# An attention and feed-forward kernel: the opening's copies, casts, loads and first up tiles rearranged

## The chip, the core and the metric

The kernel runs on one core of one Trainium2 chip. A core has five engines that run their own instruction streams in order: TensorE (matrix products, into PSUM), VectorE (DVE), ScalarE (ACT), GpSimd (POOL) and SyncE (SP), and they meet by semaphores. Transfers between memory and SBUF are issued by SP, ACT and POOL. PSUM has eight banks of 128 partitions x 512 floats.

The metric is the device time in microseconds of one execution, the median of the runs; lower is better.

## The reference

Attention with 16 query heads on 4 key and value heads, eight batches of 384 positions, head width 64; then a feed-forward layer with a squared ReLU over the 3,072 rows.

```python
k = np.repeat(k, 4, axis=1); v = np.repeat(v, 4, axis=1)
scores = np.matmul(q, k.transpose(0, 1, 3, 2)) / np.sqrt(64)
attn = softmax(scores)                                # over the keys
x = np.matmul(attn, v).transpose(0, 2, 1, 3).reshape(3072, 1024)
h = np.maximum(x @ w_in, 0.0)                         # w_in 1024 x 2048
out = h * h @ w_out                                   # w_out 2048 x 1024
```

Inputs and output are float32; the kernel casts to bfloat16 for its products.

## The kernel before

**Recording.** Every operation goes through `R.add` (L45): engine, function, tiles read and written, and an estimated cost. The recorder keeps an estimated clock per engine and per transfer queue (`ring`), derives from the tiles who waits for whom, and at the end emits each engine's operations in the order recorded (L78). The costs decide nothing on the chip except this order. The order on TensorE is chosen by the loop from L575: it collects candidates, each with the time at which it is estimated ready and a priority (score burst of batch 0: 0, transpose for q or k: 1, attention times V: 2, transpose of the output: 3, score burst of a later batch: 4, feed-forward piece: 5), and takes the ready one of lowest number, or the earliest.

**Attention, per batch.** Keys are copied twice side by side (`dup_k`, L253), so that a transpose gives the same keys on partitions 0 to 63 and 64 to 127, and two score products can run in two halves of the array. Keys and queries are turned by TensorE through PSUM and a DVE copy in batches 0 and 1 (`turn_k_pe` L278, `turn_q_pe` L293), by transposing transfers from SP later (`turn_k_dma`, `turn_q_dma`). A unit is one of 12 key blocks (4 heads x 3); its scores are 128 keys x 2 x 768 columns. In batch 0 ScalarE takes their exponentials in bursts of 1,024 columns from two pairs of banks, 0/1 and 2/3 (`burst_small`, L320: 18 bursts); later batches take two units at once from banks 0 to 5 (`burst_two`, L340: 3,072 columns). `expT` has room for eight units. `av` (L363) then makes eight pieces c per batch, each 18 small products with V, a reciprocal and a multiply on DVE; `turn_o_pe` (batch 0) or `turn_o_dma` gives x transposed, in eight chunks.

**Feed-forward, per batch.** 16 up tiles (`up_part`, L418: eight chunks of 1,024, then max on DVE and square on ScalarE) and six down tiles (`down_part`), all in banks 6 and 7. In batch 0 the first two up tiles are opened together and take the x chunks two by two as they come (`ffn`, L442).

**The opening.** `first_loads` (L207) brings the keys of head 0 on SP's queue, q of heads 0 to 3 and then the other keys on ACT's queue, all as float32. Everything else that is loaded is cast on the way and issued by POOL, in the order of L495 to L518: q and V of batch 0, three casts of keys, V's copy, three pieces of w_in (each serves two up tiles), batch 1's k, q, V, five pieces of w_in, batch 1's copies, w_out. TensorE warms up with 14 products of 256 columns (L523). DVE doubles the first keys and casts 512 columns of the first q, ACT casts 256 (L529 to L535).

**Preparing batch 2 and later.** `prepare` (L555) lists the key copy, the transposing transfers and V's copy. It is called when the batch before has all its scores issued and enough V pieces done (L586).

Of the kernel before, what the change touches and what calls it, by code (L numbers as in the profile page):

```python
# [8 lines left out]
class Recorder:  # L9
# [35 lines left out]
    def add(self, eng, fn, reads=(), writes=(), dma=None, cost=0.1, issue=0.1, rate=None):  # L45
# [20 lines left out]
        if dma is not None:  # L66
            self.clock[eng] = start + issue
            q = eng
            begin = max(self.ring.get(q, 0.0), start + issue + 0.8)
            self.ring[q] = begin + cost  # L70
            end = begin + cost + 1.2
        else:
            self.clock[eng] = start + cost
            end = start + cost + (0.2 if eng == "tensor" else 0.07)
# [59 lines left out]
def bass_gqa_attention__then__ffn_squared_relu_kernel(  # L134
# [65 lines left out]
    def load_k(b, after=()):  # L200
        st = b % NST
        R.add("gpsimd", lambda g: g.dma_start(  # L202
            k_st[st].ap().rearrange("p (g j) d -> p g (j d)", g=HKV),
            k[b].rearrange("g (p j) d -> p g (j d)", j=NJ)),
            reads=after, writes=[("k_st", st)], dma=f"k{st}", cost=1.3, issue=0.8)

    def first_loads():  # L207

        def keys(eng, g0, g1):
            R.add(eng, lambda e: e.dma_start(  # L210
                k_f32[:, g0 * NJ:g1 * NJ, :].rearrange("p (g j) d -> p g (j d)", j=NJ),
                k[0, g0:g1].rearrange("g (p j) d -> p g (j d)", j=NJ)),
                writes=[("k_f32", g) for g in range(g0, g1)], dma=f"kf{g0}", cost=0.4 * (g1 - g0), issue=0.4)

        keys("sync", 0, 1)
        R.add("scalar", lambda e: e.dma_start(
            q_f32[:, :, :], q[0, 0:4].rearrange("h (p j) d -> p h (j d)", j=NJ)),
            writes=["q_f32"], dma="qf", cost=1.3, issue=0.4)
        keys("scalar", 1, HKV)

    def load_v(b):
# [4 lines left out]
            writes=[("v_st", st)], dma=f"v{st}", cost=1.3, issue=0.8)  # L226

    def load_q(b, h0, h1):
# [4 lines left out]
            writes=[("q_st", st, h // 4, x) for h in range(h0, h1, 4) for x in range(2)], dma=f"q{st}_{h0}",  # L233
            cost=0.33 * (h1 - h0), issue=0.8)
# [18 lines left out]
    def dup_k(b, eng, g0=0, g1=HKV):  # L253
# [3 lines left out]
        R.add(eng, lambda e: e.tensor_copy(dst, src), reads=[("k_st", b % NST)] if b else [("k_f32", g) for g in range(g0, g1)],  # L257
              writes=[("k_dup", b % 2, g) for g in range(g0, g1)],
              cost=(0.15 * n / 3 + 0.1) if eng == "vector" else 0.33 * n)

    def aug_v(b, eng):
        R.add(eng, lambda e: e.tensor_copy(v_aug[b % 2][:, :, 0:D], v_st[b % NST][:, :, :]),  # L262
              reads=[("v_st", b % NST)], writes=[("v_aug", b % 2)], cost=0.4 if eng == "vector" else 2.0)

    def turn_k_dma(b):
        R.add("sync", lambda e: e.dma_start_transpose(  # L266
            out=kT[b % 2].ap(), in_=k_dup[b % 2].ap().rearrange("p n x d -> p (n x d)")),
            reads=[("k_dup", b % 2, g) for g in range(HKV)],
            writes=[("kT", b % 2, g) for g in range(HKV)], dma="turn_k", cost=2.0)

    def turn_q_dma(b, half):
# [4 lines left out]
            writes=[("qT", b % 2, 2 * half + i, x) for i in range(2) for x in range(2)], dma=f"turn_q{half}", cost=2.5)  # L276

    def turn_k_pe(b, g, banks):  # L278
# [9 lines left out]
        R.add("tensor", tr, reads=[("k_dup", b % 2, g), "ident"], writes=[("bank", i)], cost=0.18)  # L288
# [4 lines left out]
    def turn_q_pe(b, g, banks, t0=0, t1=6):  # L293
# [3 lines left out]
        parts = [h for h in range(2) if t0 < (4, 6)[h] and t1 > (0, 4)[h]]  # L297

        def tr(pe):
            for t in range(t0, t1):  # L300
# [8 lines left out]
              reads=[("bank", i)], writes=[("qT", b % 2, g, h) for h in parts], cost=0.07 + 0.068 * (t1 - t0))  # L309

    def score_reads(b, u, parts=(0, 1)):
        g = u // NJ
        return [("kT", b % 2, g)] + [("qT", b % 2, g, h) for h in parts]
# [5 lines left out]
    def burst_small(b, pieces, base):  # L320

        wide = 512 // len(pieces)

        def sc(pe):
            for n, (u, c0) in enumerate(pieces):
                for x in range(2):
                    m = pe.matmul(ps[:, base + x, n * wide:(n + 1) * wide],  # L327
                                  kT[b % 2][64 * x:64 * x + 64, u, :], q_cols(b, u // NJ, x, c0, c0 + wide))
            return m

        keys = [("bank", base), ("bank", base + 1)]
        R.add("tensor", sc, reads=[r for u, c0 in pieces for r in score_reads(b, u, (c0 // 512,))], writes=keys,
              cost=0.22 + 0.19)
        n, c0 = (b * NU + pieces[0][0]) % NEX, pieces[0][1]
        src = ps[:, base:base + 2, :].rearrange("p x (k c) -> p x k c", k=len(pieces))
        dst = expT[:, n:n + len(pieces), :, c0:c0 + wide].rearrange("p k x c -> p x k c")
        R.add("scalar", lambda e: e.activation(dst, src, AF.Exp, scale=0.125),  # L337
              reads=keys, writes=[("expT", (n + m) % NEX, c0 // 512) for m in range(len(pieces))], cost=0.92)

    def burst_two(b, u):  # L340

        def sc(pe):
            for k0, cols in ((0, ((0, 512), (512, 768))), (1, ((0, 256), (256, 768)))):
# [14 lines left out]
              reads=keys, writes=[("expT", (n + m) % NEX, h) for m in range(2) for h in range(2)], cost=2.63)  # L358

    def av_reads(b, g):  # L360
        return [("expT", (b * NU + g * NJ + j) % NEX, h) for j in range(NJ) for h in range(2)] + [("v_aug", b % 2), ("v_one", b % 2)]

    def av(b, c, banks):  # L363
# [12 lines left out]
        R.add("tensor", lambda pe: mm(pe, 6 * s2), reads=av_reads(b, g), writes=[("bank", i)], cost=0.285)  # L376
        yield
        R.add("tensor", lambda pe: mm(pe, 6 * s2 + 3), reads=av_reads(b, g), writes=[("bank", i)], cost=0.285)
# [11 lines left out]
    def turn_o_dma(b, g):  # L390
# [5 lines left out]
            dma=f"turn_o{o}", cost=2.0)  # L396
# [21 lines left out]
    def up_part(b, c, at, k0, k1):  # L418
        def piece():
            if k0 == 0:  # L420
                at.append(pick((6, 7)))
            i = at[0]

# [16 lines left out]
        return k1, need, (6, 7) if k0 == 0 else None, piece  # L440

    def ffn(b):  # L442

        opened = 2 if b == 0 else 0
        ats = [[] for _ in range(opened)]
        for k0 in range(0, NKC, 2):
            for c in range(opened):
                yield up_part(b, c, ats[c], k0, k0 + 2)
        for c in range(opened, NFC):
# [44 lines left out]
    first_loads()  # L494
    load_q(0, 4, 8)  # L495
# [7 lines left out]
    for g in range(1, HKV):  # L503
        dup_k(0, "gpsimd", g, g + 1)
    aug_v(0, "gpsimd")
    for i in range(3):
        load_w_in(i)
    load_k(1)
    load_q(1, 0, 8)
    load_q(1, 8, 16)  # L510
    load_v(1)
    for i in range(3, 8):
        load_w_in(i)
    dup_k(1, "gpsimd")
    aug_v(1, "gpsimd")
    for jj in range(2):
# [6 lines left out]
    def warm_up(pe):  # L523
        for _ in range(14):
            m = pe.matmul(bank(7)[:, 0:256], warm[:, 0:128], warm[:, :])
        return m

    R.add("tensor", warm_up, reads=["warm"], writes=[("bank", 7)], cost=2.9)
    dup_k(0, "vector", 0, 1)  # L529
    q_to = q_st[0][:, 0:4, :].rearrange("p h e -> p (h e)")  # L530
    q_from = q_f32.ap().rearrange("p h e -> p (h e)")
    R.add("vector", lambda e: e.tensor_copy(q_to[:, 0:512], q_from[:, 0:512]),
          reads=["q_f32"], writes=[("q_st", 0, 0, 0)], cost=0.6)
    R.add("scalar", lambda e: e.copy(q_to[:, 512:768], q_from[:, 512:768]),
          reads=["q_f32"], writes=[("q_st", 0, 0, 1)], cost=0.4)  # L535
# [4 lines left out]
    for u in range(NU):  # L540
        smalls.append([(u, 0)])
        if u % 2 == 1:
            smalls.append([(u - 1, 512), (u, 512)])
    turn_q = [(0, 0, "k"), (0, 0, "a"), (0, 0, "c")]
# [5 lines left out]
    units, halves, pairs, turned, up_done = 0, set(), 0, 1, -1  # L550
# [4 lines left out]
    def prepare(b):  # L555

        chores.append(([("k_st", b % NST)], lambda: dup_k(b, "gpsimd")))
        chores.append(([("k_dup", b % 2, 0), ("k_dup", b % 2, 3)], lambda: turn_k_dma(b)))
# [13 lines left out]
    f_head = next(feeding)  # L572
    av_open = None
    margin = 0.5
    while av_q or av_open or sc_q or o_q or f_head is not None:  # L575
        now = R.clock["tensor"]
        first = bool(sc_q) and sc_q[0][0] == 0
        spare = MID if first else LOW
# [7 lines left out]
        if not chores and queued < loaded and units >= queued * NU and pairs >= queued * 8:  # L586
# [7 lines left out]
        if turn_q:  # L594
            b, g, w = turn_q[0]
            src = [("k_dup", b, g)] if w == "k" else [("q_st", b, g, h) for h in range(2) if w != "ac"[1 - h]]
            cand.append((max(R.when(reads=src), open_bank(spare)), 1, "turn"))
        if av_open is not None:
            cand.append((now, 2, "av2"))
        elif av_q:  # L600
            b, c = av_q[0]
            if units >= b * NU + (c // 2 + 1) * NJ and up_done >= b - NXT:
                cand.append((max(R.when(reads=av_reads(b, c // 2)), open_bank(spare)), 2, "av"))
        if o_q:
            cand.append((max(R.when(reads=o_q[0][2]), open_bank(spare)), 3, "o"))
        if sc_q:
            b, u = sc_q[0]
            if b == 0:
                top = max(p[0] for p in smalls[u])
                ok = all((0, p[0] // NJ, p[1] // 512) in turned_g for p in smalls[u])  # L610
                ok = ok and pairs // 2 * NJ + NEX >= top + 1
                reads = [r for p in smalls[u] for r in score_reads(0, p[0], (p[1] // 512,))]
# [3 lines left out]
            else:  # L616
                ok = ((b, (u + 1) // NJ, 1) in turned_g) if b == 1 else turned >= b
# [4 lines left out]
        if f_head is not None:  # L622
# [13 lines left out]
        if what[2] == "turn":  # L636
# [3 lines left out]
            else:  # L640
                turn_q_pe(b, g, spare, *dict(q=(0, 6), a=(0, 4), c=(4, 6))[w])
            turned_g |= {(b, g, h) for h in range(2) if w in ("q", "ac"[h])}
# [18 lines left out]
        elif what[2] == "sc":  # L661
            b, u = sc_q.pop(0)
            if b == 0:
                burst_small(0, smalls[u], 2 * (u % 2))
                halves |= {(p[0], p[1] // 512) for p in smalls[u]}
# [40 lines left out]
```

The softmax here doesn't subtract the row's maximum and nothing guards it: scores larger than these inputs give would overflow.

## Time and profile before

| | us |
|---|---|
| median of 3 runs | 432.12 (431.69 to 432.97) |
| profiled execution | 432.37 |
| its span, first to last instruction | 430.6 |
| share of the span: TensorE, DVE, ACT, POOL busy | 98%, 37%, 45%, 13% |
| up products (L426), 1,024 | 174.5 busy |
| down products (L471), 758 recorded | 167.7 busy |
| exponentials: 18 of batch 0 (L337), 42 later (L357) | 16.9 and 114.5 busy |

Busy time of an engine counts an instruction from its start to its modelled end. Products overlap on TensorE, so a product's own duration (326 ns for an up product) is longer than the distance to the next one (20.80 us for 128 of them late in the kernel, or 0.1625 each). Where work stands one behind the other, the distances between starts are used. In a timeline row the numbers are start, length, engine, line, operation, tiles written and read, shape and count; in brackets stands how long the engine was idle before it and whose end released it. The first copy of the keys and other lines on GpSimd are rough.

### The profile page before, as it was taken

The numbers are of one execution on the slowest core, as the hardware profiler recorded it, in microseconds if no ns is written. First come the engines' busy times: TensorE is split into PE (matmuls) and PEld (weight loads), VectorE is DVE, ScalarE is ACT, GpSimd is POOL, SyncE is SP. The second block draws the span as 40 slices with busy tenths as digits, with TensorE's granted clock in tenths as the row PEclk, the third lists the DMA queues.
The fourth block names the chain that finished last, engine by engine and source line by source line (L and its number), as shares of the span: only waits on it lengthen the run. The fifth ranks groups of instructions, "written<-read, shape, count | busy, mean of one in ns | idle before, by whom it ended". The sixth has DMA issues, their size and how long they took to land.

```text
span 430.6 us, 7790 instructions
## 1 busy us (share of the span) xinstructions
PE 421.8 (98%) x3428; PEld 231.6 (54%) x3454; DVE 158.9 (37%) x335; ACT 194.0 (45%) x190; POOL 55.6 (13%) x68
## 2 busy tenths in 40 slices
PE   8899999999999999999999999999999999999997
PEld 4465555465454655546555455645564455446544
DVE  3474422254233543225433243533342144224412
ACT  4937750557545576455773549540241034003300
POOL 7752002404040031004000000000000000000000
DMA  8999999999596189299553230042101100110012
GB/s 147 182 195 202 190 198 215 200 191 138 105 175 156 37 137 131 85 144 166 60 103 94 70 85 0 2 106 69 49 2 49 73 26 1 50 73 26 1 63 85
DMA packets 95331, 43.90 MB, mean 102 GB/s; under 512 B 75712, under 2 KB 89280, under 8 KB 95296
## 3 DMA queue, kind: packets, MB, share of 16 engines
q0 software_dynamic: 36544, 17.44, 32.3%
q1 hardware_dynamic: 57824, 25.27, 26.4%
q10 hardware_dynamic: 928, 0.69, 0.5%
q8 instruction: 27, 0.44, 0.4%
q14 instruction: 8, 0.07, 0.1%
HBM read 35.65 MB, written 12.58 MB: 112 GB/s over the span
## 4 chain that ended last, share of the span: by engine, by line
PE 92%; ACT 3%; DMA 2%; DVE 1%; SPq 1%; issue 1%
PE ps L426 39%; PE ps L471 37%; PE ps L347 7%; PE ps L372 7%; ACT expT L337 3%; DMA qT<-q_st 1%; DMA q_f<-in_q_dram 1%; PE ps L301 1%; SPq L266 1%; DVE o_sb L387 1%; PE ps L327 0%; PE ps L285 0%; DVE qT L308 0%; DVE y_sb L480 0%; DVE rinv L381 0%
## 5 line engine op out<-in xcount | busy, mean ns | idle before, releaser
L426 PE MATMUL ps<-xT,w_in_sb 128*128 128x384 bf16 x1024 | 174.5, 326 | 0.0
L471 PE MATMUL ps<-w_out_sb,h2T 128*128 128x512 bf16 (+2 forms) x758 | 167.7, 375 | 1.7 <-issue 0.5
L357 ACT ACTIVATE expT<-ps 128x3072 bf16<-128x3072 f32 x42 | 114.5, 2725 | 70.9 <-PE ps L347 70.0
L426 PEld LDWEIGHTS ps<-xT,w_in_sb 128*128 128x128 bf16 x1024 | 97.0, 98 | 69.3 <-issue 6.2
L436 ACT ACTIVATE h2T<-hr 128x384 bf16<-128x384 f32 x128 | 64.4, 520 | 138.0 <-DVE hr L434 137.8
L471 PEld LDWEIGHTS ps<-w_out_sb,h2T 128*128 128x128 bf16 x784 | 73.6, 98 | 87.9 <-issue 6.0
L434 DVE TENSOR_SCALAR hr<-ps 128x384 f32<-128x384 f32 x128 | 71.2, 557 | 103.9 <-PE ps L426 103.9
L480 DVE COPY y_sb<-ps 128x512 f32<-128x512 f32 (+2 forms) x49 | 33.3, 681 | 130.7 <-PE ps L471 130.7
L372 PEld LDWEIGHTS ps<-v_aug,expT 128*128 128x128 bf16 x1152 | 39.8, 97 | 6.7 <-issue 0.7
L372 PE MATMUL ps<-v_aug,expT 128*128 128x65 bf16 x1152 | 41.4, 193 | 0.3 <-ACT expT L337 0.3
L387 DVE TENSOR_TENSOR o_sb<-ps,rinv 128x384 bf16<-128x384 f32 x64 | 35.6, 557 | 2.4 <-DVE rinv L381 0.2
L347 PE MATMUL ps<-qT,kT 64*128 64x512 bf16 (+1 forms) x336 | 34.6, 325 | 0.5 <-DMA qT<-q_st 0.5
L347 PEld LDWEIGHTS ps<-qT,kT 64*128 64x128 bf16 x336 | 13.0, 94 | 21.2 <-DVE o_sb L387 4.9
L381 DVE RECIPROCAL rinv<-ps 128x6 f32<-128x6 f32 x64 | 12.1, 190 | 25.5 <-PE ps L372 25.5
L337 ACT ACTIVATE expT<-ps 128x1024 bf16<-128x1024 f32 x18 | 16.9, 1070 | 2.4 <-PE ps L327 2.2
L262 POOL COPY v_aug<-v_st 128x768 bf16<-128x768 bf16 x8 | 6.6, 830 | 83.7 <-PE ps L372 67.8
L230 POOL DMA_DIRECT2D q_st<-in_q_dram x17 | 15.0, 896 | 0.9 <-POOLq L691 0.8
L257 POOL COPY k_dup<-k_st 128x1536 bf16<-128x1536 bf16 x7 | 10.3, 1469 | 37.1 <-DMA k_st<-in_k_dram 37.1
L202 POOL DMA_DIRECT2D k_st<-in_k_dram x7 | 5.3, 757 | 39.9 <-DMA qT<-q_st 39.9
L327 PE MATMUL ps<-qT,kT 64*128 64x512 bf16 (+1 forms) x48 | 7.5, 360 | 1.8 <-ACT expT L337 1.3
L240 POOL DMA_DIRECT2D w_in_sb<-in_moe_w_in_dram x8 | 7.1, 935 | 0.0
L223 POOL DMA_DIRECT2D v_st<-in_v_dram x8 | 6.3, 788 | 0.1
(26 smaller groups left out, 42.8 us busy)
## 6 DMA issues: line engine op xcount, KB each, us to landing
out_dram<-y_sb SPq DMA_DIRECT2D x47, 256.0 KB, 2.0
q_st<-in_q_dram POOLq DMA_DIRECT2D x14, 384.0 KB, 8.9
w_in_sb<-in_moe_w_in_dram POOLq DMA_DIRECT2D x8, 512.0 KB, 16.1
w_out_sb<-in_moe_w_out_dram POOLq DMA_DIRECT2D x4, 1024.0 KB, 26.4
v_st<-in_v_dram POOLq DMA_DIRECT2D x8, 192.0 KB, 9.8
k_st<-in_k_dram POOLq DMA_DIRECT2D x7, 192.0 KB, 3.9
q_st<-in_q_dram POOLq DMA_DIRECT2D x3, 192.0 KB, 5.7
xT<-o_sb SPq DMA_TRANSPOSE x28, 2.8
```

Of the source, the lines that this page charges most:

```text
L230: R.add("gpsimd", lambda g: g.dma_start(q_st[st][:, h0:h1, :], q[b, h0:h1].rearrange("h (p j) d -> p h (j d)", j=NJ)), writes=[("q_st", st ...
L337: R.add("scalar", lambda e: e.activation(dst, src, AF.Exp, scale=0.125), reads=keys, writes=[("expT", (n + m) % NEX, c0 // 512) for m in r ...
L347: m = pe.matmul(flat[:, k0 * HC + c0:k0 * HC + c1], kT[b % 2][64 * x:64 * x + 64, u + k0, :], q_cols(b, (u + k0) // NJ, x, c0, c1))
L357: R.add("scalar", lambda e: e.activation(dst, src, AF.Exp, scale=0.125), reads=keys, writes=[("expT", (n + m) % NEX, h) for m in range(2) ...
L372: m = pe.matmul(po[:, f - 6 * s2, 0:D + 1], w, v_aug[b % 2][:, g * NJ + j, 0:D + 1], start=(j == 0), stop=(j == NJ - 1))
L381: R.add("vector", lambda e: e.reciprocal(rinv[r].ap().unsqueeze(2), po[:, :, D:D + 1]), reads=[("bank", i)], writes=[("rinv", r)], cost=0.13)
L387: R.add("vector", lambda e: e.tensor_tensor(dst, srcv, rbv, ALU.mult), reads=[("bank", i), ("rinv", r)], writes=[("o_sb", o, s2)], cost=0.48)
L426: m = pe.matmul(bank(i)[:, 0:S], w_in_sb[:, kc, c * 128:(c + 1) * 128], xT[b % NXT][:, kc, :], start=(kc == 0), stop=(kc == NKC - 1))
L434: R.add("vector", lambda e: e.tensor_scalar_max(hr[r][:, :], bank(i)[:, 0:S], 0.0), reads=[("bank", i)], writes=[("hr", r)], cost=0.48)
L436: R.add("scalar", lambda e: e.activation(h2T[b % 2][:, c, :], hr[r][:, :], AF.Square), reads=[("hr", r)], writes=[("h2T", b % 2, c)], cost ...
L471: m = pe.matmul(bank(i)[:, 0:n], h2T[b % 2][:, c, i3 * 128:(i3 + 1) * 128], w_out_sb[:, c, c0:c1], start=(c == 0), stop=(c == NFC - 1))
L480: R.add("vector", lambda e: e.tensor_copy(ysl, bank(i)[:, 0:n]), reads=[("bank", i)], writes=[("y", yb)], cost=0.08 + n / 960)
```

## The change

- **First key and q.** The first key head is copied by DVE into one half and by ACT into the other. q of heads 0 to 3 comes in two transfers on ACT's queue, and ACT casts both halves (384 columns each). The other keys move from ACT's queue to SP's.
- **Warm-up.** 22 products of 128 columns, then the first key transposes, then five more.
- **Bursts of batch 0.** Units are grouped (0), (1,2), (3,4), (5,6), (7), (8,9), (10,11). Single units and the last pair use bursts of 384 columns per half (768 in all), the other pairs two of 512 and one shared one of 2 x 256. Tiles of q and of `expT` are followed in sixths, and a V piece needs only its own three sixths of its three units.
- **POOL's order.** After batch 0's loads: w_in 0, key copy of head 1, k of batch 1, key copy of heads 2 and 3, V's copy, q of batch 1, w_in 1, V of batch 1, batch 1's key copy, w_in 2 to 5, batch 1's V copy, w_in 6 and 7, w_out.
- **Early up tiles.** Four tiles of batch 0 in lanes that take single chunks. Tiles 0 and 1 use banks 6 and 7; tiles 2 and 3 may also use banks 0 to 3 once batch 0's score bursts are all issued. Batch 1's first score burst waits until no low bank is held.
- **Planner.** Batch 1's transposes get priority 4.5 and may be placed only while fewer than six V pieces of batch 0 are done or after all of x of batch 0. Transposing transfers are priced higher while POOL's queue is full, and batch 2 is prepared only after all V pieces of batch 1. Costs of copies and loads are changed.

The diff, cut to its core:

```diff
+            if shared and self.ring.get("gpsimd", 0.0) > begin:
+                self.ring["gpsimd"] += cost
+                cost = shared
...
-        keys("sync", 0, 1)
-        R.add("scalar", lambda e: e.dma_start(
-            q_f32[:, :, :], q[0, 0:4].rearrange("h (p j) d -> p h (j d)", j=NJ)),
-            writes=["q_f32"], dma="qf", cost=1.3, issue=0.4)
-        keys("scalar", 1, HKV)
+        for g0, g1 in ((0, 1), (1, HKV)):
+            R.add("sync", lambda e, g0=g0, g1=g1: e.dma_start(
+                k_f32[:, g0 * NJ:g1 * NJ, :].rearrange("p (g j) d -> p g (j d)", j=NJ),
...
+        for n in range(2):
+            R.add("scalar", lambda e, n=n: e.dma_start(
+                q_f32[:, 2 * n:2 * n + 2, :], q[0, 2 * n:2 * n + 2].rearrange("h (p j) d -> p h (j d)", j=NJ)),
...
-        opened = 2 if b == 0 else 0
-        ats = [[] for _ in range(opened)]
-        for k0 in range(0, NKC, 2):
-            for c in range(opened):
-                yield up_part(b, c, ats[c], k0, k0 + 2)
-        for c in range(opened, NFC):
+        for c in range(0 if b else EARLY, NFC):
...
+    EARLY = 4
+    early_banks = [6, 7]
+    held = set()
+    def early(c):
+        at = []
+        return [up_part(0, c, at, k0, k0 + 1, (6, 7) if c < 2 else early_banks) for k0 in range(NKC)]
...
-    for g in range(1, HKV):
-        dup_k(0, "gpsimd", g, g + 1)
+    load_w_in(0)
+    dup_k(0, 1, 2)
+    load_k(1)
+    dup_k(0, 2, 4)
     aug_v(0, "gpsimd")
-    for i in range(3):
-        load_w_in(i)
-    load_k(1)
     load_q(1, 0, 8)
     load_q(1, 8, 16)
+    load_w_in(1)
     load_v(1)
-    for i in range(3, 8):
+    dup_k(1)
+    for i in range(2, 6):
         load_w_in(i)
-    dup_k(1, "gpsimd")
     aug_v(1, "gpsimd")
+    for i in range(6, 8):
+        load_w_in(i)
...
-    dup_k(0, "vector", 0, 1)
+    R.add("vector", lambda e: e.tensor_copy(k_dup[0][:, 0:NJ, 0, :], k_f32[:, 0:NJ, :]),
+    R.add("scalar", lambda e: e.copy(k_dup[0][:, 0:NJ, 1, :], k_f32[:, 0:NJ, :]),
...
+    for n in range(2):
+        R.add("scalar", lambda e, n=n: e.copy(q_to[:, 384 * n:384 * n + 384], q_from[:, 384 * n:384 * n + 384]),
+    turn_k_pe(0, 0, (4,))
+    warm_up(5, 0.5)
...
+    for group in ((0,), (1, 2), (3, 4), (5, 6), (7,), (8, 9), (10, 11)):
+        if len(group) == 2 and group[1] < NU - 1:
+            smalls += [[(u, 0, 512)] for u in group] + [[(u, 512, 256) for u in group]]
+        else:
+            smalls += [[(u, c0, 384)] for c0 in (0, 384) for u in group]
...
-        if not chores and queued < loaded and units >= queued * NU and pairs >= queued * 8:
+        if not chores and queued < loaded and (queued - 1, NU - 1, 5) in scored and pairs >= queued * 8 + 8 * (queued == 1):
...
+        if turn_q and (b == 0 or pairs < 6 or x_done[0] == 8):
...
+            cand.append((max(R.when(reads=src), open_bank(spare)), 3.5 * b + 1, "turn"))
...
+        for n, lane in enumerate(lanes):
+            chunks, need, banks, _ = lane[0]
+            if x_done[0] >= chunks:
...
+                cand.append((t, 5 + 0.1 * n, n))
+        if f_head is not None and not lanes:
```

## The prediction

> **What bounds the kernel now.** I read four views, in this order: busy time and chain of waits on the page, busy time by stretch, the timeline of the first 31 us, and the half-microsecond stretches for the DMA rate. First the page, its parts 1 and 4:
>
> ```profile
> PE 421.8 (98%) x3428; PEld 231.6 (54%) x3454; DVE 158.9 (37%) x335; ACT 194.0 (45%) x190; POOL 55.6 (13%) x68
> ...
> PE 92%; ACT 3%; DMA 2%; DVE 1%; SPq 1%; issue 1%
> ```
>
> TensorE is busy for 421.8 of 430.6 us. All of the chain that is not TensorE has to lie in a few places. The stretches of 5 us find them (columns: stretch, length, then busy us and count for PE, PEld, DVE, ACT and POOL, clock, DMA share, GB/s):
>
> ```profile
> 5.00:10.00 5.00, 4.53 (x34) 2.56 (x34) 2.27 (x7) 3.02 (x4) 3.63 (x7) 1.00 1.22 145
> 10.00:15.00 5.00, 3.65 (x49) 1.84 (x48) 1.86 (x5) 4.56 (x6) 5.00 (x7) 1.00 1.09 139
> 15.00:20.00 5.00, 4.77 (x80) 2.90 (x76) 3.47 (x11) 5.00 (x7) 4.25 (x5) 1.00 1.47 197
> 20.00:25.00 5.00, 4.70 (x75) 2.75 (x74) 2.04 (x7) 4.43 (x5) 1.47 (x1) 1.00 1.60 191
> 25.00:30.00 5.00, 4.50 (x73) 3.54 (x69) 3.99 (x13) 0.98 (x2) 2.61 (x4) 1.00 1.48 198
> 30.00:35.00 5.00, 5.00 (x41) 2.87 (x39) 3.21 (x9) 2.21 (x2) 4.93 (x6) 1.00 1.45 197
> ```
>
> From 30 us on TensorE is full; later only one visible stall is left (0.45 us at 77.87). Between 5 and 30 us it idles 0.47+1.35+0.23+0.30+0.50 = 2.85 us, while ScalarE is nearly full from 7 to 24.4. So this is two kernels: an opening set by ScalarE's first exponentials, then 400 us of TensorE at its limit. A microsecond won before 30 us is won at the end, since everything behind is a full queue. The timeline gives the opening's marks:
>
> ```profile
> 6.94 3.08 ACT L337 ACTIVATE expT<-ps 128x1024 bf16<-128x1024 f32 x3 [1.85 <-PE ps L327]
> ...
> 10.33 12.27 ACT L337 ACTIVATE expT<-ps 128x1024 bf16<-128x1024 f32 x13 [0.30 <-PE ps L327]
> ...
> 13.80 0.74 PE L372 MATMUL ps<-v_aug,expT 128*128 128x65 bf16 x18
> ...
> 22.25 1.47 POOL L257 COPY k_dup<-k_st 128x1536 bf16<-128x1536 bf16 x1 [3.00 <-DMA k_st<-in_k_dram]
> ...
> 28.38 0.33 PE L285 MATMUL ps<-ident,k_dup 128*128 128x128 bf16 x3
> ...
> 30.40 2.11 PE L426 MATMUL ps<-xT,w_in_sb 128*128 128x384 bf16 x12
> ...
> 77.87 0.82 PE L347 MATMUL ps<-qT,kT 64*128 64x512 bf16 x8 [0.45 <-DMA qT<-q_st]
> ```
>
> Exponentials run from 6.94 to 24.43 with one gap of 0.30. The first attention-times-V piece waits until 13.80. Batch 1's keys reach GpSimd at 22.25, so its transposes stand at 28.38 to 30.40, in a stretch where TensorE has no slack. And the load queue has a hole:
>
> ```profile
> 9.50:10.00 0.50, 0.50 (x8) 0.38 (x6) 0.28 (x1) 0.50 (x1) 0.50 (x2) 1.00 0.09 10
> 10.00:10.50 0.50, 0.50 (x5) 0.17 (x3) 0.50 (x1) 0.20 (x2) 0.50 (x1) 1.00 0.00 0
> ```
>
> The last column fell from 192 at 8.0 and is back at 193 only at 12.0: some 2.5 us without loads, because GpSimd issues the first w_in piece at 8.96, behind its key and V copies.
>
> **The first chain (copies, casts, first loads).** Before: keys land at 3.53, one DVE copy of 0.55, three transposes at 4.14; q lands whole at 4.66, cast in two parts (DVE 0.43, ACT 0.41), transposes 5.16, qT copy 5.81, scores 6.29, exponential 6.94. After: DVE and ACT copy half the first key each, 0.3 to 0.36 (the 256-column ACT cast took 0.41), so the key's transposes start near 3.95 and its copy is off DVE before q comes. ACT casts q in two halves of 384 columns, 0.41 x 384/256 less a fixed part = 0.5 each. ACT has nothing queued then but the exponentials that need these casts. The gain hangs on when the first q half lands, and here a rule speaks against the change. In the trace ACT's queue ran almost alone: of about 0.18 MB in each half microsecond from 3.0 to 4.0 all was its own, so half of q (0.2 MB) would be home some 0.5 us early, at 4.1. But now the other keys (288 KB) leave ACT's queue for SP's and run beside q. The Trainium skill, "DMA: Bandwidth & Descriptors", section on queues, rings and completion order, says that each DMA engine goes round its queues packet by packet. By it the first q half shares the 360 GB/s with the keys and lands near 4.5, the second near 5.3. I take the rule, as no row has two full hardware queues side by side. Then cast to 5.0, three transposes to 5.6, copy 0.35, a 384-column score: first exponential at about 6.5, gain 0.4 (0.8 by the lone row; 0 if both halves land together at 4.9). The second half's chain ends near 7.3, when the first exponential, 0.74 long, ends.
>
> **Exponentials.** 18 of 1024 columns become 12 of 1024 and 8 of 768, over the same 18,432 columns. In the row above 13 take 12.27, so 0.944 each; the 3072-column one takes 2.725 against 1.070, so 0.81 ns a column, and 768 columns cost 0.737. Sum 12 x 0.944 + 8 x 0.737 = 17.2, against 17.0. With gaps of 0.5 they end at 6.5+17.2+0.5 = 24.2, hardly earlier than 24.43. What changes is what can run beside them: a V piece needs only its own half columns, so the first is ready after four bursts, near 10.3 instead of 13.80, and only the last of eight is left behind the last exponential, where before two were, and their chain.
>
> **Loads.** GpSimd sat idle 1.30 us until 6.71 for the keys, so the w_in issue (0.9) hides there and fills the hole. Batch 1's keys, q and V then pass two w_in pieces on the queue: at 0.19 MB/us the keys land near 14 (before 22.2), q by 18.5 (26.3). The second w_in piece lands near 21, before the up tiles 2 and 3 that need it (after 24); later pieces come 2.5 us earlier than now, and now none is waited for. GpSimd's new wait is the batch-1 key copy ahead of four w_in issues: the queue holds work until 22 by then, so nothing starves. If that cover failed, a late w_in piece would cost its lateness one for one. Splitting the key copies differently (one group, then two, with the k load between) makes groups 2 and 3 ready near 8.9, half a microsecond later than now; their scores are due near 13.5.
>
> **Batch 1's transposes and the early tiles.** The 36 transposes cost 2.0 us at 28.38. They may now run from 16 us on, between score bursts. Isolated there they cost more (three took 0.34 busy): I add 0.4. The four early up tiles are no new work; they are the same matmuls, ready while the last V chain (reciprocal 0.20, multiply 0.56, transposes, copy 0.35) runs.
>
> **TensorE's sum.** What stands between the first transposes (4.14) and the end of batch 1's (30.40), by start-to-start times of the timeline (bursts and V pieces between 13.8 and 19 us): 18 score bursts x 0.32 = 5.8; 8 V pieces x 0.66 = 5.3; batch 0's transposes 1.3+1.08+1.01+0.84 = 4.2; eight output transposes x 0.25 = 2.0; batch 1's 2.0; 16 up matmuls x 0.1625 = 2.6. Together 21.9 of 26.3, so 4.4 us were waiting. After: 21.9 + 0.2 (two more bursts, 0.1 of weight load each) + 0.4 = 22.5 from 3.95. Waiting left: about 0.8 in the first chain, where little else is ready, and 0.4 near 11 to 13, before output and w_in are there. The same state is reached at 27.65: gain **2.75**. With only 0.5 of waiting and no dearer transposes it is 3.85; with 3.0 of waiting, because a turn stands ahead of a score in the fixed order, 0.95.
>
> **The warm-up** is shortened from 14 x 256 columns (3.17 us) to 22 and later 5 of 128. The Trainium skill, "TensorE: Matmul & The Clock Gate", Part 1, has a busy window of some 3.4 us end the half-rate clock; a shorter warm-up with a hole would then be worth another 3.4 us at half rate, at most 1.7 us. But the trace shows that today's does not reach it: three transposes take 0.50 at 8.89 and 0.34 at 10.22, so full rate comes near 9.6 from the bursts after 6.3. Those stay. I take nothing.
>
> **The stall at 77.87.** Batch 2's keys landed at 66.1, behind w_out; SP's three transposes of them follow from 69.92. The load queue is 2.5 us ahead now and the planner prices these transposes higher when GpSimd's queue is full, so batch 2's scores stand later in TensorE's order. Its start after the last V piece of batch 1 costs nothing: that piece (64.91) ended with the key copy at 66.13 anyway, and the downs of batch 0 and ups of batch 1 cover it. Worth 0.45 if gone, zero if it moves along; I take 0.45.
>
> Total 2.75+0.45 = 3.2. The profiled execution took 432.37, of which 430.6 is span and 1.77 lies around it: 429.2 by its own. The median is 0.25 lower: 428.9.
>
> **The rivals.** *All fits*: ScalarE alone sets the opening, 3.85+0.45 = 4.3, 427.8; for it, TensorE's early idle; against it, that 22.5 us of work in 23 leaves no play in a fixed order. *TensorE takes over the opening*: the added transposes share two banks and DVE with the V pieces (each V piece costs DVE 1.1 us, batch 1's copies 3.6 more; DVE was busy 3.47 of 15 to 20), bursts come late, the exponentials stretch: 0.95 and the stall stays, 431.2, or 430.7 without it. *Slower*: the clock. If the shorter warm-up and chopped bursts miss the window near 9.6 and the next two, three windows of 3.4 us at half rate cost 1.7 each, 5.1 against 3.2 won: 434.0. It decides from the second missed window; against it, TensorE is busier than before from 6 to 20.
>
> **Chances.** Forecast 0.58, all fits 0.22, TensorE takes over 0.16, clock 0.04. This measurement tells about 0.3% (1.3 us) from no change. Faster: the first two and half of the third, 0.88; same 0.08; slower 0.04. The range takes in the first two, with up to 0.8 more if the lone q row holds, and most of the third: 427.0 to 431.0.
>
> **What would show it.** First exponential at 6.3 to 6.7; 20 of them, the last ending near 24.2; no dry stretch at 9 to 11.5; batch 1's transposes before that last exponential, the first V piece near 10.3; TensorE idle from 5 to 30 down from 2.85 to about 1.3; no wait for qT near 75. I am wrong if the exponentials show gaps over 1 us, if batch 1's transposes still stand behind them, or if transposes still take 0.50 for three after 10 us.

## The result and the profile after

| | before | changed |
|---|---|---|
| median, us | 432.21 (431.69 to 432.97, 4 runs) | 430.01 (429.93 to 430.71, 4 runs) |
| ratio, 95% interval | | 0.9951 [0.9933, 0.9970] |
| span of the profiled execution | 430.6 | 428.1 |
| batch 0's exponentials: first starts, last ends | 6.94, 24.43 | 6.59, 24.63 |
| batch 1's first score burst | 32.45 | 30.60 |

The change wins 2.2 us where 3.2 were forecast; the profiled spans differ by 2.5. The page of the changed kernel, parts 1, 2 and 4 (the second row is the clock that TensorE was granted, in tenths, over 40 slices of 10.7 us; the page of before has no such row):

```profile
PE 423.2 (99%) x3467; PEld 232.2 (54%) x3467; DVE 158.8 (37%) x334; ACT 194.9 (46%) x194; POOL 55.1 (13%) x67
...
PEclk8999999999999999999999999999999999999999
...
PE 98%; DMA 1%; ACT 0%; DVE 0%; ACTq 0%; issue 0%
```

The chain is TensorE all through, and ScalarE's 3% of before has left it. That does not yet mean that ScalarE sets nothing: the chain follows what ended last, and a TensorE that is kept busy with cheap or slow work looks full. The first slice of the clock, 8, is new. The stretches show where it lies (columns as before: PE, PEld, DVE, ACT, POOL busy, clock, DMA share, GB/s):

```profile
5.00:10.00 5.00, 3.75 (x29) 1.64 (x30) 1.95 (x5) 3.92 (x6) 5.00 (x8) 0.81 1.51 182
10.00:15.00 5.00, 5.00 (x69) 3.11 (x67) 3.13 (x8) 4.41 (x5) 3.84 (x5) 0.85 1.54 191
15.00:20.00 5.00, 5.00 (x72) 2.84 (x71) 2.78 (x9) 4.84 (x7) 3.33 (x4) 1.00 1.53 196
20.00:25.00 5.00, 4.93 (x88) 3.28 (x88) 3.10 (x9) 4.50 (x6) 2.87 (x4) 1.00 1.47 198
25.00:30.00 5.00, 5.00 (x64) 3.66 (x61) 4.77 (x14) 0.39 (x1) 5.00 (x7) 1.00 1.46 197
```

TensorE's idle time from 5 to 30 us is 1.25+0.07 = 1.32, against 2.85. The dry stretch of the load queue is gone: the last column stays between 182 and 198. The clock is below 1.00 in two stretches; in steps of half a microsecond it is 1.00 up to 8.0, 0.50 from 8.5 to 11.0 and 1.00 again from 11.5. By these shares the drop lasts from about 8.1 to 11.5. The timeline of the changed kernel has the marks:

```profile
3.71 0.48 PE L286 MATMUL ps<-ident,k_dup 128*128 128x128 bf16 x3
...
5.96 0.33 PE L302 MATMUL ps<-ident,q_st 128*128 128x128 bf16 x3 [1.03 <-ACT q_st L551]
6.22 0.34 PE L328 MATMUL ps<-qT,kT 64*128 64x384 bf16 x2
...
6.59 4.35 ACT L338 ACTIVATE expT<-ps 128x768 bf16<-128x768 f32 x5 [0.78 <-PE ps L328]
...
8.30 0.61 PE L328 MATMUL ps<-qT,kT 64*128 64x512 bf16 x2
8.84 0.50 PE L286 MATMUL ps<-ident,k_dup 128*128 128x128 bf16 x3
9.27 0.61 PE L328 MATMUL ps<-qT,kT 64*128 64x256 bf16 x4
9.81 0.82 PE L302 MATMUL ps<-ident,q_st 128*128 128x128 bf16 x6
10.43 0.53 PE L286 MATMUL ps<-ident,k_dup 128*128 128x128 bf16 x3
10.89 0.61 PE L328 MATMUL ps<-qT,kT 64*128 64x512 bf16 x2
11.43 0.52 PE L302 MATMUL ps<-ident,q_st 128*128 128x128 bf16 x6
...
11.54 7.03 ACT L338 ACTIVATE expT<-ps 128x1024 bf16<-128x1024 f32 x8 [0.59 <-PE ps L328]
...
12.20 0.74 PE L374 MATMUL ps<-v_aug,expT 128*128 128x65 bf16 x18
...
15.52 0.39 PE L328 MATMUL ps<-qT,kT 64*128 64x256 bf16 x4
15.84 0.72 PE L374 MATMUL ps<-v_aug,expT 128*128 128x65 bf16 x18
...
16.77 0.34 PE L286 MATMUL ps<-ident,k_dup 128*128 128x128 bf16 x3
...
26.56 0.50 PE L302 MATMUL ps<-ident,q_st 128*128 128x128 bf16 x6
...
27.90 2.76 PE L431 MATMUL ps<-xT,w_in_sb 128*128 128x384 bf16 x16
...
78.36 0.82 PE L349 MATMUL ps<-qT,kT 64*128 64x512 bf16 x8
```

TensorE waits 1.03 us for the cast of q's second half, with the first score burst behind that wait. Six transposes take 0.82 at 9.81 and 0.50 at 26.56. A score burst takes 0.54 from its start to the next one's at 8.30, 9.27 and 10.89, and 0.32 at 15.52. A gap of 0.59 in the exponentials follows the slow ones. Three of batch 1's eight transpose groups run beside the exponentials (16.77, 19.50, 21.20); five stand behind them, from 26.56. Batch 2's first scores at 78.36 carry no bracket: the stall of before is gone.

The recorded clock shows only part of the half-rate time. At 3.71 three transposes take 0.48, against 0.34 at 16.77, and the record says 1.00. The kernel before has the same, here with the half microsecond around its row:

```profile
8.89 0.50 PE L285 MATMUL ps<-ident,k_dup 128*128 128x128 bf16 x3
...
8.50:9.00 0.50, 0.50 (x6) 0.12 (x3) 0.50 (x1) 0.38 (x2) 0.50 (x2) 1.00 1.08 127
```

So "half rate" below is read from the length of equal instructions, and a recorded 1.00 does not rule it out.

### The profile page after: what moved, and what is told of

Same layout as the page of the kernel before. It is cut to its first block, busy times and chain, and to the rows that moved or that the text cites. A ratio compares the mean times of both kernels' runs of the same rounds, so it can differ in the third digit from the quotient of the medians.

```text
span 428.1 us, 7844 instructions
## 1 busy us (share of the span) xinstructions
PE 423.2 (99%) x3467; PEld 232.2 (54%) x3467; DVE 158.8 (37%) x334; ACT 194.9 (46%) x194; POOL 55.1 (13%) x67
## 4 chain that ended last, share of the span: by engine, by line
PE 98%; DMA 1%; ACT 0%; DVE 0%; ACTq 0%; issue 0%
PE ps L431 40%; PE ps L480 39%; PE ps L374 9%; PE ps L349 7%; PE ps L328 1%; DMA q_f<-in_q_dram 1%; PE ps L302 1%; PE ps L407 0%; PE ps L286 0%; ACT expT L338 0%; DVE o_sb L389 0%; ACT q_st L551 0%; ACTq L218 0%; DVE y_sb L489 0%; DVE rinv L383 0%
## 5 line engine op out<-in xcount | busy, mean ns | idle before, releaser
L480 PE MATMUL ps<-w_out_sb,h2T 128*128 128x512 bf16 (+2 forms) x784 | 172.0, 375 | 0.0
L349 PE MATMUL ps<-qT,kT 64*128 64x512 bf16 (+1 forms) x336 | 34.6, 325 | 0.0
L338 ACT ACTIVATE expT<-ps 128x1024 bf16<-128x1024 f32 (+1 forms) x20 | 17.2, 941 | 1.7 <-PE ps L328 1.5
L258 POOL COPY k_dup<-k_st 128x1536 bf16<-128x1536 bf16 x7 | 10.3, 1467 | 36.7 <-DMA k_st<-in_k_dram 36.7
L328 PE MATMUL ps<-qT,kT 64*128 64x384 bf16 (+2 forms) x48 | 8.0, 360 | 0.3 <-DVE qT L309 0.2
```

Source lines behind the costliest of these rows:

```text
L328: mm = pe.matmul(ps[:, base + x, m * wide:(m + 1) * wide], kT[b % 2][64 * x:64 * x + 64, u, :], q_cols(b, u // NJ, x, c0, c0 + wide))
L349: m = pe.matmul(flat[:, k0 * HC + c0:k0 * HC + c1], kT[b % 2][64 * x:64 * x + 64, u + k0, :], q_cols(b, (u + k0) // NJ, x, c0, c1))
L480: m = pe.matmul(bank(i)[:, 0:n], h2T[b % 2][:, c, i3 * 128:(i3 + 1) * 128], w_out_sb[:, c, c0:c1], start=(c == 0), stop=(c == NFC - 1))
```

## The experiments

The times are medians of four executions (before and changed) or of five and more, each group run beside the kernel before; the ratio is to that kernel. It came out between 431.88 and 432.21 in these groups, so times of different groups compare to about 0.3 us, and ratios are the better measure; e1, e6, e7 and e8 are one group. "ScalarE's end" is the end of batch 0's last exponential in the profiled execution, and the last column is the span less that.

| run | us | ratio, interval | span | ScalarE's end | rest |
|---|---|---|---|---|---|
| before | 432.21 | | 430.6 | 24.43 | 406.2 |
| changed | 430.01 | 0.9951 [0.9933, 0.9970] | 428.1 | 24.63 | 403.5 |
| e1_score_first | 429.31 | 0.9945 [0.9932, 0.9957] | 427.3 | 23.81 | 403.5 |
| e6_old_warm | 430.02 | 0.9960 [0.9947, 0.9973] | 428.0 | 24.45 | 403.6 |
| e7_fill | 429.14 | 0.9936 [0.9922, 0.9949] | 427.3 | 23.82 | 403.5 |
| e8_fill_first | 429.59 | 0.9941 [0.9928, 0.9953] | 427.8 | 24.28 | 403.5 |
| f5_old_prepare | 429.29 | 0.9931 [0.9920, 0.9943] | 427.5 | 24.07 | 403.4 |
| e9_keys_behind_q | 431.62 | 0.9992 [0.9984, 1.0000] | 430.2 | 26.73 | 403.5 |
| g1_q_on_sp_first | 431.81 | 0.9996 [0.9988, 1.0004] | 430.5 | 26.99 | 403.5 |
| h1_old_bursts | 429.42 | 0.9942 [0.9929, 0.9955] | 428.0 | 24.24 | 403.8 |
| f4_two_tiles | 429.67 | 0.9948 [0.9935, 0.9961] | 427.8 | 23.69 | 404.1 |
| h2_bursts_tiles | 430.16 | 0.9954 [0.9941, 0.9967] | 428.3 | 24.16 | 404.1 |
| f3_old_pool | 430.98 | 0.9973 [0.9962, 0.9983] | 429.2 | 23.59 | 405.6 |
| b1_pool_alone | 434.17 | 1.0048 [1.0030, 1.0067] | 431.5 | 23.21 | 408.3 |

The table is the main finding. In the changed kernel and in seven variants of it the rest is 403.4 to 403.6, while ScalarE's end moves over 3.2 us. So the opening ends with ScalarE's last exponential, although the chain on the page names only TensorE. That does not say what moves this end: in e9 and g1 ScalarE waits for late scores. The row of e7 below settles it for the kernels with little waiting: from 6.67 on ScalarE has no gap there, and its own work sets the end. What an edit is worth falls into two parts: what it does to ScalarE's end, and what it does to the rest.

**The opening's order and clock.**

e1_score_first: the first score burst goes ahead of the transposes of q's second half.

```diff
-        if turn_q and (b == 0 or pairs < 6 or x_done[0] == 8):
+        if turn_q and (b == 0 or pairs < 6 or x_done[0] == 8) and not (w == "c" and sc_q[0] == (0, 0)):
```

> The change with one edit: TensorE's order has the first score burst before the transposes of q's second half (in the changed kernel it stood behind them and waited from 5.0 to 5.96 for their cast). Theory A (the fixed order holds up the first exponential, and ScalarE sets the opening): first exponential at 5.7 to 5.8 instead of 6.59, last exponential ends near 23.9 instead of 24.63, time 0.5 to 0.8 us below the changed kernel's 430.0. Theory B (from 6 us on TensorE is full and sets the opening): first exponential earlier all the same, but the time falls by 0.3 at most.

e6_old_warm: the old warm-up block.

```diff
-                m = pe.matmul(bank(7)[:, 0:128], warm[:, 0:128], warm[:, 0:128])
+                m = pe.matmul(bank(7)[:, 0:256], warm[:, 0:128], warm[:, :])
-    warm_up(22, 2.5)
+    warm_up(14, 2.9)
-    warm_up(5, 0.5)
```

> The change with the old warm-up: 14 products of 256 columns in one block, none behind the first key's transposes. Theory A (the stretch at half clock from 8.2 to 11.5 comes from the new, shorter and split warm-up): the clock is not at 0.50 after 8 us, and the time falls by 0.5 to 1.2 us. Theory B (half rate for some windows of the opening whatever the warm-up; only where it falls differs): transposes at half rate up to 9 or 10 us as before the change, time within 0.4 us of the changed kernel.

e7_fill: products into the hole from 5 to 6 us. e8_fill_first has this and e1's edit.

```diff
             turned_g |= {(b, g, t) for t in range(6) if w in ("q", "ac"[t // 3])}
+            if w == "a":
+                warm_up(12, 0.0)
```

> The change with 12 more warm-up products of 128 columns right behind the first three transposes of q, in the hole from 5.0 to 5.96. Theory A (TensorE's hole at 5 to 6 us brings the half-rate stretch from 8.2 to 11.5): that stretch is gone, the exponentials' gap of 0.59 at 10.94 is gone, time 0.5 to 1.2 us lower. Theory B (the stretch comes from the low density of the work from 6 to 8.2, or from the phase of the window): it stays, time within 0.3 us.

> Both edits: the first score burst ahead of q's second half, and 12 warm-up products behind the first three transposes of q. If order and clock both count, the gains add: first exponential at 5.8, no half-rate stretch after 8 us, time 1.0 to 1.8 us below the changed kernel. If TensorE is full from 6 us and the clock's windows fall as they like, within 0.4 us of it.

The exponentials of e7_fill, then of e1_score_first, and two rows of TensorE in e6_old_warm, from their timelines:

```profile
6.67 17.15 ACT L338 ACTIVATE expT<-ps 128x768 bf16<-128x768 f32 x20 [0.86 <-PE ps L328]
```

```profile
5.74 0.80 ACT L338 ACTIVATE expT<-ps 128x768 bf16<-128x768 f32 x1
7.06 10.68 ACT L338 ACTIVATE expT<-ps 128x768 bf16<-128x768 f32 x12 [0.52 <-PE ps L328]
17.91 5.90 ACT L338 ACTIVATE expT<-ps 128x1024 bf16<-128x1024 f32 x7 [0.17 <-PE ps L328]
```

```profile
7.26 0.50 PE L286 MATMUL ps<-ident,k_dup 128*128 128x128 bf16 x3
...
9.51 0.34 PE L286 MATMUL ps<-ident,k_dup 128*128 128x128 bf16 x3
```

e7 starts no earlier than the changed kernel but runs its 20 exponentials without a gap: 17.15, against 24.63-6.59 = 18.04. No half-rate stretch is left after 8 us, and the five executions (428.98 to 429.56) lie below all four of the changed kernel and below all five of e6, which ran beside it. Theory A holds: the gain is 0.9 by the times, 0.6 by the ratios. e1 starts 0.85 earlier, then meets a gap of 0.52, since the second burst waits for q's second half; it too has no half-rate stretch in its profile. Its median is 0.7 lower, but by the ratios that is 0.3, and two of its five executions (430.09 and 430.22) are no faster than the changed kernel: whether its order alone wins is open. In e6 three transposes at 7.26 still take 0.50, as before the change; the first full-speed ones stand at 9.51, and the time is that of the changed kernel: theory B. In e8 the 12 products, at half rate, last from 4.82 to 6.31 and hold the score burst up until 6.23; the two edits get in each other's way, and with 0.4 won the gains do not add.

What brings the half-rate stretch is not settled. TensorE was busy 2.07 of the 3.4 us ahead of it (4.8 to 8.2) in the changed kernel, 3.10 in e7, but 2.11 in e1, which did not have it. It also moves between executions: e1 and the changed kernel have the same products up to 4.5 us, and the five short ones behind the first key's transposes took 0.47 in one and 0.74 in the other. The mean clock recorded for an execution is 0.996 in five of the nine executions of the changed kernel and e6, and 1.00 in all 37 with the filling products (e7, e8, the f and h runs). Two of the changed kernel's four show no recorded drop and were no faster (spans 428.2 and 428.9); since the record can miss half rate, as in e6's profile with 1.00 throughout, it does not tell whether these two ran at full rate.

**The queues of the first loads.** e9_keys_behind_q has e1's edit and the keys of heads 1 to 3 behind both halves of q on ScalarE's queue. g1_q_on_sp_first has e1's edit and SyncE's queue with the first key, q's second half and then the other keys.

```diff
-        for g0, g1 in ((0, 1), (1, HKV)):
-            R.add("sync", lambda e, g0=g0, g1=g1: e.dma_start(
...
+        keys("sync", 0, 1)
...
+        keys("scalar", 1, HKV)
```

```diff
+        keys(0, 1)
+        for n, eng in ((0, "scalar"), (1, "sync")):
+            R.add(eng, lambda e, n=n: e.dma_start(
...
+        keys(1, HKV)
```

> The change with the first score burst ahead of q's second half, and with the keys of heads 1 to 3 back on ScalarE's queue behind both halves of q (no filling products). Theory A (sharing the engines with those keys delays q's second half from about 4.6 to 5.3, and ScalarE's end plus 403.5 us is the span): second half of q at 4.5 to 4.7, first exponential at 5.7 to 5.9, no gap of 0.5 behind it, ScalarE's end near 23.1 to 23.4, span 426.6 to 427.0. Theory B (TensorE, or the clock, sets the opening now): span not under 427.2.

> The change with the first score burst ahead of q's second half, and SyncE's queue carrying the first key, then q's second half, then the other keys (ScalarE's queue q's first half alone). Theory A (whichever stands first on the queues lands first; ScalarE's end plus 403.5 us is the span): second half of q near 4.5, the other keys by 6.0, first exponential at 5.7 to 5.9 and none of the 0.5 gap behind it, ScalarE's end near 23.3, span near 426.8, time near 428.6. Theory B (a third transfer on a queue starts late, as with the keys behind q on ScalarE's queue, landed at 8.4): keys after 7.5, GpSimd waits for them, span over 428.5.

Both went wrong in the same way. ScalarE, GpSimd and TensorE of e9, then GpSimd of g1:

```profile
3.92 1.08 ACT L554 CAST q_st<-q_f 128x384 bf16<-128x384 f32 x2
...
10.75 1.02 ACT L341 ACTIVATE expT<-ps 128x1024 bf16<-128x1024 f32 x1 [1.31 <-PE ps L331]
```

```profile
8.46 0.50 POOL L261 CAST k_dup<-k_f 128x384 bf16<-128x384 f32 x1 [2.33 <-DMA k_f<-in_k_dram]
```

```profile
10.93 0.85 PE L305 MATMUL ps<-ident,q_st 128*128 128x128 bf16 x6
...
13.17 0.51 PE L305 MATMUL ps<-ident,q_st 128*128 128x128 bf16 x6
```

```profile
7.55 0.50 POOL L261 CAST k_dup<-k_f 128x384 bf16<-128x384 f32 x1 [1.42 <-DMA k_f<-in_k_dram]
```

In e9 both casts of q run back to back, so q's second half was there by 4.4 and not at 5.3: the first half of theory A is right. But the keys, third on their queue, came at 8.46; in the changed kernel their cast started at 6.09 without waiting. The next heads' scores were late, and 2.3 us were lost against e1. The batch-1 load chain behind the keys on GpSimd moved with them. Not all of the loss is the queue's: TensorE ran at half rate up to about 13 us in e9, as the six transposes show, and its first exponential came at 6.32 and not at 5.74. In g1 six transposes still took 0.82 at 12.79. How the loss divides is not known. g1 went as its theory B said. For e9 the number of theory B came true (430.2 is not under 427.2), but ScalarE's end plus 403.5 is the span once more, which was theory A's sum.

**The rest: parts taken out of e7.** f3_old_pool puts GpSimd's old order back; f4_two_tiles has `EARLY = 2`; f5_old_prepare drops `+ 8 * (queued == 1)`; h1_old_bursts has the old grouping:

```diff
+    for u in range(NU):
+        smalls.append([(u, 0, 512)])
+        if u % 2 == 1:
+            smalls.append([(u - 1, 512, 256), (u, 512, 256)])
```

h2_bursts_tiles is h1 and f4 together.

> The changed kernel with the 12 filling products (429.1, span 427.3, last exponential of batch 0 ends at 23.8), but with GpSimd's order of before: the key and V copies first, then three w_in pieces, then batch 1's loads, its copies last. Theory A (the new order's worth is the few batch-1 transposes and up products that it lets run beside the exponentials): ScalarE's end stays at 23.8, the eight transposes all stand behind it, time up by 0.7 to 1.2 us. Theory B (it is most of the whole gain, since batch 1's late q also holds up the stretch behind the exponentials): up by 1.5 to 2.5 us. If TensorE has as much to do either way: within 0.3.

> The changed kernel with the 12 filling products, but with two early up tiles instead of four (none in the score banks). Theory A (tiles 2 and 3 fill TensorE's holes behind the last exponential): holes of 0.3 to 0.8 us between 23.8 and 28, time up by as much. Theory B (batch 1's transposes that are left fill them): time within 0.2 us.

> The changed kernel with the 12 filling products, but batch 2 is prepared under the old condition (eight V pieces done, not sixteen). Theory A (the later preparation took the 0.45 us stall of before at 77.87 away): TensorE waits 0.3 to 0.6 us for qT near 75, time up by that. Theory B (the load queue, 2.5 us ahead, and the higher prices of the transposing transfers did): no wait, time within 0.2.

> The changed kernel with the 12 filling products, but with the old grouping of batch 0's bursts (18 of 1,024 columns, one for each unit and one for each pair). Theory A (the grouping shortens the stretch behind the last exponential, since one V piece and its chain is left there and not two): ScalarE's end within 0.4 us of 23.8, but 0.5 to 1.0 us more between it and batch 1's first score burst than with the new groups, time up by that. Theory B (TensorE has other work to put there): time within 0.3 us.

> The changed kernel with the 12 filling products, with the old bursts and with two early tiles together (each alone cost: bursts 0.7 of span, of which 0.4 is ScalarE's later end; tiles 0.5). If the two act on the same holes behind the last exponential, the sum is more than additive, 1.4 to 2.0 us, as each covers for the other. If additive: 1.1 to 1.3, span 428.4 to 428.6.

TensorE in f3 and in f4, the one row of each behind ScalarE's end where it stood still:

```profile
77.22 0.82 PE L349 MATMUL ps<-qT,kT 64*128 64x512 bf16 x8 [1.64 <-DMA qT<-q_st]
```

```profile
28.21 0.83 PE L349 MATMUL ps<-qT,kT 64*128 64x512 bf16 x8 [0.45 <-DVE qT L309]
```

f3 loses 1.9 us of span, in theory B's range but not for its reason: 1.64 of it is one wait for batch 2's q, because that batch's transposing transfers stand behind loads which end later again (its key copy starts at 65.12, against 63.17 in e7) while the kernel ahead of them stays faster than before. In the opening the old order costs only 0.3. f4 shows the hole that tiles 2 and 3 fill: theory A, 0.5. f5, whose transposing transfers for batch 2 do start earlier (64.49 against 65.61), has no stall and the same time: theory B; its span is 0.2 longer because its q came later in that execution and ScalarE ended at 24.07. h1 moves ScalarE's end by 0.4 (the first exponential needs all of q: it starts at 7.63) and the rest by 0.3, in time 0.3 us. h2 loses 1.0 in span and in time, where the parts lost 1.2 in span and 0.8 in time: they add.

**One part alone.** b1_pool_alone is the kernel before with the new order of loads and copies on GpSimd.

> The kernel before with the new order of GpSimd's loads and copies as its only edit (the batch-1 transposes then come up among batch 0's bursts in its order). Theory A (the forecast's: what is won is the batch-1 transposes moved beside the exponentials, 1.6 to 2.0 us, and the stall at 77.87): time near 429.6 to 430.2. Theory B (in the opening the loads alone win little, since TensorE has no free time there once V pieces wait for pairs of units; what they prevent is the stall that a faster opening would meet at batch 2): 0.3 to 0.8 below 432.1, the stall at 77.87 gone.

TensorE of b1, the last of batch 1's transposes, the V pieces behind them, and batch 2's first scores:

```profile
22.86 0.50 PE L301 MATMUL ps<-ident,q_st 128*128 128x128 bf16 x6
23.26 2.42 PE L372 MATMUL ps<-v_aug,expT 128*128 128x65 bf16 x72
...
75.38 0.82 PE L347 MATMUL ps<-qT,kT 64*128 64x512 bf16 x8 [2.47 <-DMA qT<-q_st]
```

Both theories missed: the edit alone makes the kernel slower, 1.0048 [1.0030, 1.0067]. All eight groups of batch-1 transposes did start before ScalarE's end (the last at 22.86), with four V pieces left behind it, and batch 1's scores began at 28.30 instead of 32.45. But attention then ran into the loads: batch 2's scores stand in the order where TensorE was free at 72.91 (77.42 in the kernel before), their data were there at 75.38, and TensorE waited 2.47 us instead of 0.45. That the planner's old prices placed them so early is likely, but the prices were not changed alone. In that execution 2.0 us of stall stand against about 1.1 won before. Its executions also spread more than any others' (432.42 to 435.73), and what moved them is not known.

## Why the prediction was right or wrong

The time, 430.01, lies in the range, and the sign and the kind of gain are as forecast. The size was 2.2 and not 3.2, and two of the prediction's three signs of being wrong came true: batch 1's transposes stood behind the exponentials for five of eight groups, and three transposes took 0.53 at 10.43. The range was wide enough to hold these misses. By its steps:

- **What bounds the opening.** Right that it is ScalarE's exponentials; the rest of 403.5 in eight runs, with e7's row without a gap, shows it more sharply than the prediction said it. Its own sum, though, was made on TensorE's work, and so took TensorE as the limit. The two sums lay close (24.2 for ScalarE's end, 27.65 for TensorE's mark), which hid that.
- **The first chain.** Predicted 6.5, measured 6.59, by two errors that cancel: the hit is luck. By the arbitration rule of the Trainium skill ("DMA: Bandwidth & Descriptors", section on queues, rings and completion order) the first half of q was to land at 4.5; ScalarE began its cast at 3.82. The second half came at 5.3, as computed, and by 4.4 where the keys were taken off (e9): sharing with the keys does delay it. Even sharing step by step was not seen (last section), so that the 5.3 fits may be luck too. But then TensorE's order, not q, held the first score until 6.22; in e1 the exponential started at 5.74.
- **Exponentials.** The sum of 17.2 is what e7 measured (17.15). In the changed kernel they took 18.04, with 0.75 of gaps where 0.5 were allowed for, and the end came at 24.63 and not 24.2. The first V piece came at 12.20 and not near 10.3 (e7 11.40, e1 10.60).
- **The clock: the term that was mis-sized.** For the shorter warm-up itself "I take nothing" was right: with the old one in the changed kernel (e6) the time is 430.02. The miss lies in the sum, which prices every score burst at 0.32, its distance at full rate. In the changed kernel three bursts took 0.54, and all 20 together, from start to next start less the standing still, about 6.9 where 6.0 were reckoned. The kernel before had slow bursts as well (about 6.5 for its 18, not 5.8): of the 4.4 us that the prediction booked as waiting, TensorE stood still for 3.2, and the rest was slow work that the change did not take away. e7, with the pause filled, spends about 6.3 on the bursts, and its profiled span is 3.3 below that of before. That this is close to the 3.2 of the forecast shows what full rate is worth here; it does not confirm the forecast, since e7 has an edit more.
- **Batch 1's transposes.** All were to run beside the exponentials; three groups of eight did. This planner's order put the others behind; why is not shown. That they can fit is shown by b1, whose order left four V pieces behind instead.
- **TensorE's sum.** The state reckoned at 27.65 was reached near 28.4: at 27.90 thirteen of the sixteen up products were done, and three more take 0.5. That is 2.0 instead of 2.75. The slow bursts are the largest piece of the miss.
- **Loads.** Right that they end the dry stretch and land earlier: batch 1's keys by 13.41, where 14 was forecast, and batch 2's by 63.12 against 66.13. Their worth was put in the wrong place: in the opening f3 puts it at 0.3, but without them the faster opening would have met a stall of 1.64 at batch 2.
- **The stall at 77.87.** Right, 0.45. The early loads are needed: without them it is 1.64 (f3). They do not suffice: with them in the old kernel, old prices included, it is 2.47 (b1). The prices were not tested alone. The later condition for preparing batch 2 did nothing: without it the stall is zero too (f5).
- **The early tiles.** They were booked as cover; f4 gives them 0.5.

The rest shrank by 2.7 from before to after. The stall is 0.45 of it; tiles, bursts and loads, each undone alone in e7, move the rest by 0.6, 0.3 and 0.5 (f3's 405.6 less its stall of 1.64). Some 0.9 is not split further: it was not tried to undo the finer tracking of q and of the exponentials by sixths, which lets a V piece start on its own columns.

The best versions run are e7_fill, the change with 12 more filling products (429.14, ratio 0.9936 [0.9922, 0.9949]), and f5, the same within the noise.

## What to carry to other kernels

When two engines both look full, compare variants: if the span follows one engine's milestone with a constant rest, the stage ends there, whatever the chain on the page names. Whether that engine's own work sets the milestone, or what feeds it, its gaps tell: none in e7, 1.31 us at one place in e9. A faster opening brings the whole program earlier to the next transfer, so ask for each queue what its next landing is, and whether it moves too: the same load order was worth 0.3 us in the opening, prevented 1.64 later, and alone made the kernel slower. And an order that is fixed in advance is only as good as its estimates: the first score burst stood 0.9 us behind a transfer that the planner thought would land earlier.

## What the runs showed of the hardware

- TensorE's granted clock fell from full to half rate from about 8.1 to 11.5 us, though its longest pause before was 1.03 us. The Trainium skill ("TensorE: Matmul & The Clock Gate", Part 1) has the rate fall after an idle window of some 3.4 us. The drop lasted that long, but TensorE was busy for 2.07 of the 3.4 us from 4.8 to 8.2; here the measurement decides. With the pause filled the drop was not there, and neither was it in e1, at 2.11 of 3.4. What decides is open.
- When full rate comes differs between executions with the same warm-up. Three key transposes took 0.50 at 8.89 in the kernel before, but 0.34 at 7.35 in b1, which has the same 14 products in front:

```profile
7.35 0.34 PE L285 MATMUL ps<-ident,k_dup 128*128 128x128 bf16 x3 [0.57 <-POOL k_dup L257]
```

- The recorded clock can read 1.00 at half rate: in e9 it is 1.00 from 0 to 13 us, while six transposes took 0.85 at 10.93 and 0.51 at 13.17.
- A third transfer on a hardware queue, with GpSimd's loads running beside it, came late. The 288 KB of keys behind both halves of q on ScalarE's queue came at 8.46 (e9, by the cast that waits for them), and third on SyncE's at 7.55 (g1); second on SyncE's they were there by 6.09. In the kernel before, second on ScalarE's queue behind q in one piece, they came at 6.71. In e9 ScalarE's queue moved only 8 packets between 4.0 and 4.5, and 39 to 109 in each half microsecond from 4.5 to 7.0. GpSimd's loads also began to move earlier in e9 and g1 (between 3.0 and 3.5, against 4.0 and 4.5 in the kernel before and the changed one), so the place on the queue is not separated from that.
- Two hardware queues side by side did not share evenly step by step. Packets of ScalarE's (q10) and SyncE's queue (q1) in the changed kernel, from 2.5 to 3.0 and from 3.0 to 3.5; from 3.5 to 4.0 they were 97 and 147:

```profile
q10 hardware_dynamic: 170, 0.12, 74.1%
q1 hardware_dynamic: 59, 0.04, 31.0%
...
q1 hardware_dynamic: 174, 0.13, 79.1%
q10 hardware_dynamic: 62, 0.04, 25.5%
```
